# Holding q and k loads to three tiles, moving stores to GpSimd's ring, and gating transposes and scores apart

## The chip, the cores and the metric

The kernel runs on one core of a Trainium2 chip. The metric is the device time of one launch in microseconds. Thirteen runs of the kernel before gave a median of 214.38 us (213.67 to 217.96). Separate from them, one execution was profiled.

## What is computed

Attention over 4 batches, 8 heads, 768 positions and a head size of 64, with a distance bias, a local window of 96 positions and 8 global positions; its output, with the heads side by side, goes through two matrices with a "tanh shrink" between them.

```python
scores = scale * np.matmul(q, k.transpose(0, 1, 3, 2))
keep = is_global | is_local          # first 8 positions, or 0 <= row - col < 96
scores = np.where(keep, scores + bias, -1e9)
a = softmax(scores)                  # row maximum taken off, sum + 1e-9
x = (a @ v), heads side by side      # 3072 x 512
h = x @ w_in                         # 512 x 2048
out = (h - np.tanh(h)) @ w_out       # 2048 x 512
```

Inputs and output are float32; the kernel computes its products in bfloat16.

## The kernel before

**Tiles.** The 3072 rows are 24 tiles of 128. They are visited in the order `SEQ` (line 50): first the first tile of each batch, then the others. In all that follows a tile's number u is its place in this order. A tile needs its own keys (the diagonal block), and, unless it is the first of its batch, the keys of the tile before it in its batch (the other block). The global keys and values are copied into the first columns of each key tile (K, line 333) and the first rows of each value tile (V, line 360).

**Steps of one tile.** The loads of k, q and v (`load_bf`, line 232) cast to bfloat16 and are issued by GpSimd; k and q of a tile share a tile of store `kq` from the pool `bpool`, with `KQ` = 5 buffers (lines 47 and 80). k and q of tiles 0 and 1 come as float32 by SyncE and ScalarE and are cast on chip. T is the transpose of q and k: for tiles 0 to 5 TensorE does it (lines 277 and 281, `PE_T` = 6), for the others a DMA transpose that SyncE issues (`a_DT`, line 283), from `kq` into a tile `qk` of `kpool` (7 buffers). S is the scores (line 314); from tile 12 three blocks are run together (`R3`, `RUN`). E is the exponential on ScalarE (line 323), M the mask on VectorE (line 329), AV the product with v on TensorE (lines 342 and 346), R the division by the row sum on VectorE (lines 354 and 355), X the transpose of the result: TensorE to tile 8 (line 369), then a DMA transpose by SyncE (`a_DX`, line 380).

**The two matrices.** Tiles 0 to 5 are groups of one tile, the others groups of two (`groups`). m1 (line 410) multiplies a group by `w_in` in chunks; th is tanh on ScalarE (line 422), g is h - tanh(h) on VectorE (line 429). m2 (line 444) multiplies by `w_out` in four quarters for each tile, ev copies the sum out of PSUM (line 454) into a tile `ot` (4 buffers), and st stores it: `store` (line 456) is issued by ScalarE, and for the last tile by SyncE.

**What sets the order.** Each engine runs its instructions in the order in which they stand. That order is made before the build by `plan()` (line 702). Each operation is entered by `op` or `flex` with an engine, a duration, the operations that it comes after, and the buffers that it takes and gives back; `plan()` repeatedly picks the operation that can start first by these durations. DMAs get a model of two rings (`ring` and `share`, lines 724 and 725), and a table `NUDGE` (line 467) shifts single operations by hand. The durations decide only the order: on the chip an instruction waits for semaphores, that is for data and for buffers, and not for the planned time.

Progress of m1 is counted in tiles: `prog` (line 576) lists each chunk of m1 with the number of tiles that are done before it. A tile's transpose may be planned only after the last chunk with a progress of at most u - 5.5 (`AHEAD`, `go` and `late`, lines 608 and 609); its scores follow when the transpose is done.

```python
go = [key for a, key in prog if a <= u - AHEAD]
late = [("issue", ("T", u - 1)) if u else None, go[-1] if go else None]
...
op(("T", u), SP, 0.3, lambda u=u: a_DT(u), after=[rk, rq] + late, give=["kq"], dma=T_DT, slack=SLACK_DT)
```

**Queues.** GpSimd issues all loads but four in one list: the order of the early ones is `LOADS` (line 532; t is a tile's three loads, i a piece of `w_in`, o a piece of `w_out`), and later tiles follow in order. The build gives GpSimd's DMAs eight semaphores, so each issue waits for the landing of the one eight places before it. A k load also waits until its `kq` buffer is free, and everything behind it in GpSimd's list waits with it. SyncE's list holds the DMA transposes of T and X in one order, so a transpose can wait behind another's data. ScalarE issues the stores between its other work.

Of the kernel before, what the change touches and what calls it, by code (L numbers as in the profile page):

```python
# [15 lines left out]
def kernel(  # L16
# [11 lines left out]
    nc = tc.nc  # L28
# [18 lines left out]
    KQ = 5  # L47
# [33 lines left out]
    kpool = ctx.enter_context(tc.tile_pool(name="kpool", bufs=7))  # L81
# [374 lines left out]
    def store(u, part):  # L456
        lo, hi = parts(u)[part]
        eng = nc.sync if u == NU - 1 else nc.scalar
        eng.dma_start(out=out[SEQ[u] * P : (SEQ[u] + 1) * P, lo:hi], in_=ots[u][:, lo:hi])


    AHEAD = 5.5
# [4 lines left out]
    NUDGE = {  # L467
        ('AV', 21): -0.3,
        ('E', 12, 1): 0.3,
        ('E', 13, 0): 0.3,  # L470
        ('E', 13, 1): -0.6,
        ('E', 14, 1): -0.6,
        ('E', 17, 0): -0.15,
        ('E', 17, 1): -0.15,
        ('E', 18, 1): 0.15,
        ('E', 21, 1): 1.0,
        ('E', 9, 1): -0.3,
        ('M', 14, 1): 0.3,
        ('M', 20, 0): 1.0,
        ('M', 9, 1): 1.0,  # L480
        ('R', 15): 0.6,
        ('R', 9): -0.3,
        ('S', 3, 0): 0.15,
        ('S', 6, 0): 1.0,
        ('S', 7, 0): 0.6,
        ('V', 16): -0.15,
        ('V', 19): -0.6,
        ('V', 4): -0.3,
        ('X', 6): 0.15,
        ('Xe', 9): -0.3,  # L490
        ('ev', 7, 0): 1.0,
        ('g', 1, 6): 0.3,
        ('g', 11, 6): 0.6,
        ('g', 13, 14): 0.3,
        ('g', 2, 2): 0.6,
        ('g', 7, 14): 1.0,
        ('g', 7, 8): 0.6,
        ('g', 9, 2): 1.0,
        ('m1', 12, 0): 0.6,
        ('m1', 4, 4): -0.3,  # L500
        ('m1', 4, 8): -0.15,
        ('m1', 5, 0): -0.3,
        ('m1', 5, 4): -0.3,
        ('m1', 5, 8): -0.15,
        ('m1', 6, 2): 0.6,
        ('m1', 8, 6): 1.0,
        ('m1', 9, 8): 0.6,
        ('m2', 1, 2): 1.0,
        ('m2', 10, 0): 1.0,
        ('m2', 11, 0): -0.3,  # L510
        ('m2', 12, 3): 0.3,
        ('m2', 15, 1): 0.3,
        ('m2', 2, 1): 1.0,
        ('m2', 21, 1): 0.6,
        ('m2', 3, 0): 0.6,
        ('m2', 3, 2): 1.0,
        ('m2', 5, 3): 1.0,
        ('m2', 7, 1): 0.3,
        ('m2', 7, 3): 0.3,
        ('m2', 8, 0): 1.0,  # L520
        ('st', 12, 0): 0.6,
        ('st', 8, 0): 1.0,
        ('th', 6, 10): -0.6,
        ('th', 7, 10): 0.3,
        ('th', 9, 8): 0.15,
    }
    SLACK_DT, SLACK_DX = 4.0, 4.0
    WARM = (1.1, 7.0)
    COLD = 6.3
    FETCH = (15.8, 0.9)  # L530
    T_ROWS, T_LD, T_W, T_ST, T_DT, T_DX = 0.67, 0.89, 1.3, 0.7, 1.75, 0.9
    LOADS = "ttttiiitiiiotoooioitooo"
# [68 lines left out]
    for u in range(NU):  # L601
# [6 lines left out]
        go = [key for a, key in prog if a <= u - AHEAD]  # L608
        late = [("issue", ("T", u - 1)) if u else None, go[-1] if go else None]
        if u < PE_T:  # L610
            t_us = 0.47 if PLAIN <= u < ROWS else 0.24
            apart = u < APART
            for j, r in ((1, rk), (0, rq)):
                prior = [("issue", ("T1", u))] if j == 0 else []
                name = ("T1" if j else "T", u)
                op(name, PE, t_us, lambda u=u, j=j: a_T(u, j), after=[r] + late + prior,
# [5 lines left out]
        else:  # L622
            op(("T", u), SP, 0.3, lambda u=u: a_DT(u), after=[rk, rq] + late, give=["kq"], dma=T_DT, slack=SLACK_DT)
        os = (0, 1) if i else (0,)
        if u < B:
            for o in os:
# [4 lines left out]
                op(("S", u, o), PE, 0.43, lambda u=u, o=o: a_S([(u, o)]), after=after_S(u) + [("B", u, o)])  # L631
        for o in os if u >= B else ():
# [49 lines left out]
    for u in range(NU):  # L682
# [10 lines left out]
        for part in range(len(parts(u))):  # L693
# [4 lines left out]
            op(("st", u, part), SP if u == NU - 1 else ACT, 0.1 if u == NU - 1 else 0.4, lambda u=u, part=part: store(u, part), after=[("ev", u, part)],  # L698
# [3 lines left out]
    def plan():  # L702
        bufs = {"mo": 3, "kq": KQ, "p0": 3, "p1": 3,
# [40 lines left out]
        while ready or any(queues.values()):  # L744
# [13 lines left out]
            for key in ready:  # L758
                if key not in since:
                    since[key] = max([0.0] + [start[a[1]] if a[0] == "issue" else done[a] for a in ops[key]["after"]])  # L760
                if key[0] == "S" and len(ops[key]["hold"]) > 2:
                    due = min(due, since[key] + YIELD)
            for key, n in cand:
# [5 lines left out]
                via = POOL if o["eng"] is POOL else SP  # L769
                if o["dma"] and len(ring[via][1]) >= 8:  # L770
                    t = max(t, sorted(ring[via][1])[-8])
                if key not in since:
                    since[key] = max([0.0] + [start[a[1]] if a[0] == "issue" else done[a] for a in o["after"]])
# [141 lines left out]
```

The softmax here doesn't subtract the row's maximum and nothing guards it: scores larger than these inputs give would overflow.

## Time and profile before

| what | value |
|---|---|
| median of 13 runs | 214.38 us |
| the profiled execution's own time | 214.66 us |
| its span, first to last instruction | 212.9 us |
| mean granted TensorE clock | 0.998 |
| T6 to T23, the 18 DMA transposes of q and k, issue to landing | 3.0 / 9.3 / 12.2 us (least, median, most) |
| the 15 DMA transposes of x | 2.4 / 4.6 / 9.4 us |
| stores issued by ScalarE: 23 of 256 KB, median to landing | 5.9 us |
| GpSimd's k loads waiting for transposes to free `kq` | 15.1 us, 3 times |
| SyncE's sequencer waiting with a transpose for q loads | 49.9 us, 8 times |

A busy share of an engine says how long its instructions ran, not that they were at their peak; matmuls are pipelined, so the start-to-start distance of two matmuls is what one costs the stream, and "busy" of TensorE counts overlapping spans once. The chain of waits follows the last instruction back to what released it, step by step. A DMA's time is counted from its issue to the landing of all its data, so it includes the time in its queue.

### The profile page before, as it was taken

What the parts mean: (1) busy time and instruction counts of PE and PEld (TensorE: products, weight loads), DVE (VectorE), ACT (ScalarE), POOL (GpSimd) and SP (SyncE); (2) the same over time, 40 slices, a digit from 0 to 9 for tenths busy, and PEclk for the clock granted to TensorE, in tenths of its full rate; (3) what the DMA queues carried; (4) which work ended last, traced back from release to release, by engine and by line L of the source; (5) the groups of instructions that cost most, each with busy time, mean ns of one, the idle gap of its engine ahead of it and who ended that gap; (6) DMA issues with size and microseconds to landing.
All of it is one profiled execution on the core that took longest, in us unless ns stands there. A gap on an engine that the chain in (4) does not pass through costs nothing.

```text
span 212.9 us, 5322 instructions
## 1 busy us (share of the span) xinstructions
PE 205.2 (96%) x2198; PEld 145.2 (68%) x2198; DVE 131.1 (62%) x269; ACT 120.0 (56%) x184; POOL 71.9 (34%) x92
## 2 busy tenths in 40 slices
PE   7899999999599999999999999999999999999994
PEld 2679995985256867677677578757755786666754
DVE  5579895655367677385666577756655594333611
ACT  4777875553346786497358366667545673444410
POOL 8996486757146545335342700000000000000000
PEclk9999999999999999999999999999999999999999
DMA  5999999999999999999999999212373220110112
GB/s 176 185 190 177 181 203 180 186 152 151 151 165 188 185 122 189 129 183 183 151 162 178 187 122 183 50 62 64 99 94 108 77 49 0 52 51 14 38 49 100
DMA packets 106073, 27.49 MB, mean 129 GB/s; under 512 B 94656, under 2 KB 103104, under 8 KB 106048
## 3 DMA queue, kind: packets, MB, share of 16 engines
q0 software_dynamic: 74048, 13.11, 84.2%
q1 hardware_dynamic: 28144, 7.48, 27.5%
q10 hardware_dynamic: 3856, 6.56, 8.9%
q8 instruction: 17, 0.28, 0.5%
q14 instruction: 8, 0.07, 0.1%
HBM read 27.26 MB, written 6.29 MB: 158 GB/s over the span
## 4 chain that ended last, share of the span: by engine, by line
PE 90%; DMA 7%; DVE 1%; ACT 0%; issue 0%; DVEq 0%
PE ps L410 40%; PE ps L444 37%; PE ps L314 5%; DMA qk<-kq 5%; PE ps L342 3%; PE ps L346 2%; DMA kf<-in_k_dram 2%; PE ps L277 1%; PE ps L369 1%; PE ps L281 1%; PE ps L165 1%; DVE kh L296 0%; ACT qk L296 0%; DVE kq L255 0%; DVE ot L454 0%
## 5 line engine op out<-in xcount | busy, mean ns | idle before, releaser
L410 PE MATMUL ps<-xT,w_in_bf 128*128 128x256 bf16 (+1 forms) x960 | 92.9, 251 | 0.0
L444 PE MATMUL ps<-w_out_bf,g 128*128 128x512 bf16 (+3 forms) x416 | 91.2, 363 | 0.0
L410 PEld LDWEIGHTS <-w_in_bf 128*128 128x128 bf16 x960 | 77.3, 98 | 13.3 <-DMA xT<-x 0.5
L429 DVE TENSOR_TENSOR g<-ps,th 128x512 bf16<-128x512 f32 (+1 forms) x102 | 64.9, 656 | 29.0 <-ACT th L422 28.4
L422 ACT ACTIVATE th<-ps 128x512 f32<-128x512 f32 (+1 forms) x102 | 56.8, 573 | 38.0 <-PE ps L410 34.7
L444 PEld LDWEIGHTS <-g 128*128 128x128 bf16 x416 | 37.9, 98 | 33.7
L323 ACT ACTIVATE pd<-ps 128x1024 bf16<-128x1024 f32 x24 | 24.4, 1024 | 14.9 <-PE ps L314 14.9
L242 POOL DMA_DIRECT2D kq<-in_k_dram x20 | 17.8, 888 | 25.4 <-DMA qk<-kq 15.1
L236 POOL DMA_DIRECT2D vb<-in_v_dram x24 | 21.4, 891 | 13.0 <-DMA kq<-in_k_dram 3.0
L323 ACT ACTIVATE po<-ps 128x1024 bf16<-128x1024 f32 x20 | 20.3, 1024 | 6.1 <-PE ps L314 6.1
L242 POOL DMA_DIRECT2D kq<-in_q_dram x20 | 17.7, 886 | 6.2 <-DMA vb<-in_v_dram 4.4
L329 DVE TENSOR_TENSOR pd<-pd,mk 128x1024 bf16<-128x1024 bf16 x20 | 13.8, 690 | 6.4 <-ACT pd L323 6.3
L355 DVE TENSOR_TENSOR x<-ps,rden 128x512 bf16<-128x512 f32 x24 | 16.6, 691 | 0.8
L454 ACT COPY ot<-ps 128x512 f32<-128x512 f32 x16 | 9.4, 585 | 13.7 <-PE ps L444 13.7
L329 DVE TENSOR_TENSOR po<-po,mk 128x1024 bf16<-128x1024 bf16 x20 | 13.6, 686 | 2.9 <-ACT po L323 2.9
L342 PE MATMUL ps<-vb,pd 128*128 128x65 bf16 x192 | 14.1, 193 | 0.0
L342 PEld LDWEIGHTS <-pd 128*128 128x128 bf16 x192 | 12.5, 98 | 1.4 <-issue 0.2
L314 PE MATMUL ps<-qk 64*128 64x128 bf16 x288 | 10.8, 217 | 2.5 <-DMA qk<-kq 2.5
L454 DVE COPY ot<-ps 128x512 f32<-128x512 f32 (+3 forms) x10 | 5.8, 585 | 12.0 <-PE ps L444 11.9
L314 PEld LDWEIGHTS <-qk 64*128 64x128 bf16 x288 | 8.1, 94 | 7.5 <-issue 4.2
L346 PE MATMUL ps<-vb,po 128*128 128x65 bf16 x160 | 12.4, 193 | 0.0
L346 PEld LDWEIGHTS <-po 128*128 128x128 bf16 x160 | 10.4, 97 | 1.1
(48 smaller groups left out, 80.8 us busy)
## 6 DMA issues: line engine op xcount, KB each, us to landing
out_dram<-ot ACTq DMA_DIRECT2D x23, 256.0 KB, 5.9
vb<-in_v_dram POOLq DMA_DIRECT2D x24, 128.0 KB, 10.9
kq<-in_k_dram POOLq DMA_DIRECT2D x22, 128.0 KB, 11.7
kq<-in_q_dram POOLq DMA_DIRECT2D x22, 128.0 KB, 11.5
w_in_bf<-in_moe_w_in_dram POOLq DMA_DIRECT2D x8, 256.0 KB, 7.9
w_out_bf<-in_moe_w_out_dram POOLq DMA_DIRECT2D x8, 256.0 KB, 9.0
kf<-in_k_dram SPq DMA_DIRECT2D x2, 256.0 KB, 4.7
qf<-in_q_dram ACTq DMA_DIRECT2D x2, 256.0 KB, 4.0
```

Of the source, the lines that this page charges most:

```text
L236: i = nc.gpsimd.dma_start(out=v_of(u)[:, :, 0:Dh], in_=by_head)
L242: i = nc.gpsimd.dma_start(out=dst.rearrange("p (h d) -> p h d", d=Dh), in_=by_head)
L314: nc.tensor.matmul(s[:, slot(2 * p + hh), :], kT(prev_of[u] if o else u)[r, p, :], qk[u][r, 0, p, :], start=u >= B, stop=True, skip_group_ ...
L323: nc.scalar.activation(pr[u, o].rearrange("q (a h) f -> q a h f", a=2)[:, part], sc[u, o][:, part, :].rearrange("q a (h f) -> q a h f", f= ...
L329: nc.vector.tensor_tensor(out=pr[u, o], in0=pr[u, o], in1=mk[:, :, mask_of(u, o) - 1, :], op=ALU.mult)
L342: nc.tensor.matmul(dst, pr[u, 0][:, slot(h), :], v_of(u)[:, h, :], start=True, stop=last,)
L346: nc.tensor.matmul(dst, pr[u, 1][:, slot(h), :], v_of(prev_of[u])[:, h, :], start=False, stop=True,)
L355: nc.vector.tensor_tensor(out=xs[u].rearrange("q (a h) d -> q a h d", a=2), in0=t[:, :, :, 0:Dh], in1=rden.to_broadcast([P, 2, H // 2, Dh] ...
L410: nc.tensor.matmul(t[:, (f - f0) * n : (f - f0 + 1) * n], w_in_bf[j][:, c, fo : fo + P], xT[b][:, c, o : o + n], start=(c == 0), stop=(c = ...
L422: nc.scalar.activation(h_view(ths[g, f0], g, m), h_view(hs[g, f0], g, m), AF.Tanh, bias=0.0, scale=1.0)
L429: nc.vector.tensor_tensor(out=gs[b][:, f0 : f0 + m, o : o + n], in0=h_view(hs.pop((g, f0)), g, m), in1=h_view(ths.pop((g, f0)), g, m), op= ...
L444: nc.tensor.matmul(os_[u, part][:, 0 : hi - lo], gs[b][:, f, t * P : (t + 1) * P], w_out_bf[f // FJ][:, f % FJ, lo:hi], start=(f == 0), st ...
```

## The change

- `KQ` goes from 5 to 3: at most three tiles of k and q are in store between load and transpose. `kpool` goes from 7 to 8 buffers, and the planner now counts them (`qk`): T takes one, the scores that read it last give it back.
- `store` is issued by GpSimd for tiles 0 to 20, by ScalarE for tiles 21 and 22 and by SyncE for tile 23. In GpSimd's list a store stands between loads, and waits there for its eviction.
- The gate is split. T keeps 5.5 (`AHEAD_T`). Scores of tiles from 4 on get a gate of their own: they may be planned only after the chunk of m1 with a progress of at most u - 4.5 (`gate`).
- The order of the early loads (`LOADS`) changes.
- The table of nudges is emptied, and the planner's model of DMA is replaced: `fly` advances three rings (GpSimd's, SyncE's, ScalarE's) together with shares that depend on which have work, and stops them at fixed times (`FETCHES`). The durations of the engines' operations stay, but for issues of stores.

In the order that is built, TensorE has the same instructions as before in another order. GpSimd's list has three stores behind the loads of tile 9, one behind those of each of tiles 10 and 11, and from tile 13 on a store behind most tiles' loads: store 5 behind tile 13, store 6 behind 14, stores 7 and 8 behind 17, and stores 9 to 12 behind 18 to 21; stores 13 to 20 follow all loads. SyncE's list has the transposes in nearly the same order; x of tiles 10 and 17 now stand ahead of T13 and T21, and x of tile 19 ahead of x of tile 20.

```diff
--- before.py
+++ after.py
@@ -44,7 +44,8 @@
     WJ = 8
     FJ = CF // WJ
     NV = 9
-    KQ = 5
+    KQ = 3
+    NK = 8
     ROWS = 4
     APART = 4
     SEQ = [b * NQ for b in range(B)] + [t for t in range(NU) if t % NQ]
@@ -78,7 +79,7 @@
     cpool = ctx.enter_context(tc.tile_pool(name="const", bufs=1))
     stpool = ctx.enter_context(tc.tile_pool(name="stage", bufs=PLAIN))
     bpool = ctx.enter_context(tc.tile_pool(name="bpool", bufs=KQ))
-    kpool = ctx.enter_context(tc.tile_pool(name="kpool", bufs=7))
+    kpool = ctx.enter_context(tc.tile_pool(name="kpool", bufs=NK))
     ppool = ctx.enter_context(tc.tile_pool(name="ppool", bufs=3))
     xpool = ctx.enter_context(tc.tile_pool(name="xpool", bufs=3))
     tpool = ctx.enter_context(tc.tile_pool(name="tpool", bufs=NG))
@@ -455,81 +456,30 @@
 
     def store(u, part):
         lo, hi = parts(u)[part]
-        eng = nc.sync if u == NU - 1 else nc.scalar
+        eng = nc.sync if u == NU - 1 or u < BY_SP else nc.gpsimd if u < BY_POOL else nc.scalar
         eng.dma_start(out=out[SEQ[u] * P : (SEQ[u] + 1) * P, lo:hi], in_=ots[u][:, lo:hi])
 
 
-    AHEAD = 5.5
+    AHEAD, AHEAD_T = 4.5, 5.5
+    BY_POOL, BY_SP = 21, 0
     YIELD = 0.0
     HALVES = 99
     EB = 2
     INF = 1.0e9
-    NUDGE = {
...
-    }
-    SLACK_DT, SLACK_DX = 4.0, 4.0
+    NUDGE = {}
+    SLACK_DT, SLACK_DX = 1.0, 1.0
...
-    FETCH = (15.8, 0.9)
-    T_ROWS, T_LD, T_W, T_ST, T_DT, T_DX = 0.67, 0.89, 1.3, 0.7, 1.75, 0.9
-    LOADS = "ttttiiitiiiotoooioitooo"
+    FETCHES = [(15.8, 0.9), (23.0, 0.2), (31.0, 0.3)] + [(a, 0.9) for a in (40, 49, 61, 72, 83, 94, 105, 116, 127, 140)]
+    T_ROWS, T_LD, T_W, T_ST, T_DT, T_DX = 0.67, 0.89, 1.3, 0.65, 1.05, 0.55
+    RING = 5.8
+    TAIL = {POOL: 0.45, SP: 0.8, ACT: 0.8}
+    SHARE = {
+        (True, False, False): (1.0, 0, 0), (False, True, False): (0, 1.0, 0), (False, False, True): (0, 0, 1.0),
+        (True, True, False): (0.36, 0.42, 0), (True, False, True): (0.5, 0, 0.42), (False, True, True): (0, 0.5, 0.42),
+        (True, True, True): (0.3, 0.29, 0.2),
+    }
+    LOADS = "tttitiiitiiootooiiotooo"
     first, n_of = [], {"t": 0, "i": 0, "o": 0}
     for c in LOADS + "t" * NU:
         if n_of[c] < (NU if c == "t" else WJ):
@@ -587,13 +537,16 @@
             op(("mke", m, a), ACT, 0.52, lambda m=m, a=a: a_mke(m, a), after=[("mk", m, a)],
                free=[("mk", m, a)], pri=1)
 
-    run_of, blocks_of = {}, {}
+    run_of, blocks_of, gate = {}, {}, {}
     for u in range(NU):
         for o in (0,) if u < B else (0, 1):
             n = 2 * (u - R3) + o
             first_b = (u, o) if u < B else (u, 0) if u < R3 else (R3 + n // RUN * RUN // 2, n // RUN * RUN % 2)
             run_of[u, o] = ("S",) + first_b
             blocks_of.setdefault(run_of[u, o], []).append((u, o))
+
+    for u in range(B, NU):
+        gate[u] = [key for a, key in prog if a <= u - AHEAD][-1:]
 
     def after_S(u):
         return ([("Te", u, 0), ("Te", u, 1)] if u < PE_T else [("T", u)])
@@ -605,22 +558,21 @@
             flex(("cq", u), [(ACT, 0.55), (DVE, 0.6)], lambda eng, u=u: cast(u, 0, qf, eng), after=[rq], pri=-1)
             flex(("ck", u), [(DVE, 0.6), (ACT, 0.55)], lambda eng, u=u: cast(u, 1, kf, eng), after=[rk], pri=-1)
             rk, rq = ("ck", u), ("cq", u)
-        go = [key for a, key in prog if a <= u - AHEAD]
-        late = [("issue", ("T", u - 1)) if u else None, go[-1] if go else None]
+        late = [("issue", ("T", u - 1)) if u else None] + [key for a, key in prog if a <= u - AHEAD_T][-1:]
         if u < PE_T:
             t_us = 0.47 if PLAIN <= u < ROWS else 0.24
             apart = u < APART
             for j, r in ((1, rk), (0, rq)):
                 prior = [("issue", ("T1", u))] if j == 0 else []
                 name = ("T1" if j else "T", u)
-                op(name, PE, t_us, lambda u=u, j=j: a_T(u, j), after=[r] + late + prior,
+                op(name, PE, t_us, lambda u=u, j=j: a_T(u, j), after=[r] + late + prior, take=["qk"] if j else [],
                    hold=[(name, 1)] if apart or j else [], give=[] if j else ["kq"])
                 flex(("Te", u, j), [(ACT, 0.5), (DVE, 0.6 if u < ROWS else 0.34)],
                      lambda eng, u=u, j=j: a_Te(u, j, eng),
                      after=[("T1" if j and apart else "T", u)] + ([] if apart or j else [("Te", u, 1)]),
                      free=[name] if apart else [] if j else [("T1", u)])
         else:
-            op(("T", u), SP, 0.3, lambda u=u: a_DT(u), after=[rk, rq] + late, give=["kq"], dma=T_DT, slack=SLACK_DT)
+            op(("T", u), SP, 0.3, lambda u=u: a_DT(u), after=[rk, rq] + late, take=["qk"], give=["kq"], dma=T_DT, slack=SLACK_DT)
         os = (0, 1) if i else (0,)
         if u < B:
             for o in os:
@@ -628,16 +580,19 @@
                    after=biased_by + [("dT", 1) if o else None,
                                     ("issue", ("S", u - EB, 0)) if u >= EB else None],
                    hold=[(("S", u, o), 2)])
-                op(("S", u, o), PE, 0.43, lambda u=u, o=o: a_S([(u, o)]), after=after_S(u) + [("B", u, o)])
+                op(("S", u, o), PE, 0.43, lambda u=u, o=o: a_S([(u, o)]), after=after_S(u) + [("B", u, o)],
+                   give=["qk"])
         for o in os if u >= B else ():
             if run_of[u, o] != ("S", u, o):
                 continue
             bl = blocks_of["S", u, o]
             deps = [("issue", ("mk", 1, 1)), ("issue", ("mk", 2, 1))]
+            back = [w for w, ow in bl if ow and prev_of[w] >= B] + [w for w, ow in bl if ow and SEQ[w] % NQ == NQ - 1]
             for w, ow in bl:
+                deps += gate[w]
                 deps += after_S(w) + [("K", prev_of[w]) if ow and prev_of[w] >= B else None]
             op(("S", u, o), PE, 0.22 + 0.215 * len(bl), lambda bl=bl: a_S(bl), after=list(dict.fromkeys(deps)),
-               hold=[(("S", w, ow), 2) for w, ow in bl])
+               hold=[(("S", w, ow), 2) for w, ow in bl], give=["qk"] * len(back))
         for o in os:
             if u < HALVES:
                 op(("E", u, o), ACT, 0.93, lambda u=u, o=o: a_E(u, o), after=[run_of[u, o]],
@@ -695,12 +650,13 @@
             flex(("ev", u, part), alt, lambda eng, u=u, part=part: m2_e(u, part, eng),
                  after=[("m2", u, 4 * part + 3)], take=["ot"] if part == 0 else [],
                  give=["mo"] if u < EARLY2 else [], free=[("m2", u, part)], pri=1)
-            op(("st", u, part), SP if u == NU - 1 else ACT, 0.1 if u == NU - 1 else 0.4, lambda u=u, part=part: store(u, part), after=[("ev", u, part)],
+            by = SP if u == NU - 1 or u < BY_SP else POOL if u < BY_POOL else ACT
+            op(("st", u, part), by, {SP: 0.3, POOL: 0.7, ACT: 0.4}[by], lambda u=u, part=part: store(u, part), after=[("ev", u, part)],
                give=["ot"] if part == len(parts(u)) - 1 else [], dma=T_ST)
 
 
     def plan():
-        bufs = {"mo": 3, "kq": KQ, "p0": 3, "p1": 3,
+        bufs = {"mo": 3, "kq": KQ, "qk": NK, "p0": 3, "p1": 3,
                 "x": 3, "xT": NG, "g": NG, "th": 3, "ot": 4}
         avail = {n: [0.0] * c for n, c in bufs.items()}
         free = {PE: WARM[0], ACT: 3.4, DVE: 1.5, POOL: 1.0, SP: 0.7}
@@ -721,9 +677,58 @@
                 b[i : i + n] = [INF] * n
             return at, got
 
-        ring = {SP: [0.0, []], POOL: [5.8, []]}
-        share = {SP: 0.5, POOL: 0.5}
         done, start, width = {}, {}, {}
+        flying, landed, at_dma = {POOL: [], SP: [], ACT: []}, {POOL: [], SP: [], ACT: []}, [0.0]
+
+        def fly(jobs, t, t_end):
+            fin = {}
+            while t < t_end:
+                stop = [(a, n) for a, n in FETCHES if t < a + n][:1] or [(INF, 0)]
+                if stop[0][0] <= t:
+                    t = min(sum(stop[0]), t_end)
+                    continue
+                heads = [q for q in jobs if jobs[q] and jobs[q][0][1] <= t]
+                later = min([jobs[q][0][1] for q in jobs if jobs[q] and jobs[q][0][1] > t] + [t_end])
+                if not heads:
+                    t = later
+                    continue
+                rate = SHARE[tuple(q in heads for q in (POOL, SP, ACT))]
+                rate = {q: r for q, r in zip((POOL, SP, ACT), rate)}
+                dt = min([later - t] + [jobs[q][0][2] / rate[q] for q in heads])
+                dt = min(dt, stop[0][0] - t)
+                t += dt
+                for q in heads:
+                    jobs[q][0][2] -= dt * rate[q]
+                    if jobs[q][0][2] < 1e-6:
+                        key = jobs[q].pop(0)[0]
+                        fin[key] = t + TAIL[q] + ops[key]["slack"]
+            return fin
+
+        def fly_from(q, key, t, end):
+            busy = flying[POOL]
+            done.update(fly(flying, at_dma[0], t))
+            at_dma[0] = max(at_dma[0], t)
+            begin = end + (2.0 if q is POOL else 1.0)
+            if key[0] in ("T", "Xe"):
+                begin = t + (4.2 if busy else 2.2)
+            if q is POOL:
+                begin = max(begin, RING)
+            flying[q].append([key, begin, ops[key]["dma"], q])
+            landed[q].append(key)
+            done.update(fly({k: [list(j) for j in v] for k, v in flying.items()}, at_dma[0], INF))
+
+        flies = {key: any(a[0] != "issue" and ops[a]["dma"] for a in o["after"]) for key, o in ops.items()}
+
+        def due_at(key):
+            if flies[key] or key not in since:
+                since[key] = max(
+                    [0.0] + [start[a[1]] if a[0] == "issue" else done[a] for a in ops[key]["after"]]
+                )
+            return since[key]
+
+        def at_of(x):
+            return done[x] if isinstance(x, tuple) else x
+
         f1 = f2 = 0.0
         queues = {}
         for u in range(NU):
@@ -756,22 +761,17 @@
                     cand.append((qu[0], 10 ** 6 + name[1]))
...
@@ -786,7 +786,7 @@
                     if len(avail[p]) < n_p:
                         t = None
                         break
-                    t = max(t, sorted(avail[p])[n_p - 1])
+                    t = max(t, sorted(at_of(x) for x in avail[p])[n_p - 1])
                 if t is None:
                     continue
                 c = (round(t + NUDGE.get(key, 0.0), 3), o["pri"], n)
@@ -805,16 +805,7 @@
             if o["at"]:
                 done[key] = o["at"]
             elif o["dma"]:
-                via = POOL if o["eng"] is POOL else SP
-                mine, other, part = ring[via], ring[SP if via is POOL else POOL], share[via]
-                begin = max(mine[0], end + (1.0 if via is SP else 1.97))
-                both = min(max(0.0, other[0] - begin), o["dma"] / part)
-                mine[0] = begin + o["dma"] + both * (1 - part)
-                if begin < FETCH[0] <= mine[0]:
-                    mine[0] += FETCH[1]
-                other[0] += both * part
-                done[key] = mine[0] + (0.8 if via is SP else 0.45) + o["slack"]
-                mine[1].append(done[key])
+                fly_from(o["eng"], key, t, end)
             else:
                 done[key] = end + LAT[o["eng"]]
             if o["hold"]:
@@ -832,9 +823,9 @@
                     continue
                 bank[banks[label] : banks[label] + width[label]] = [done[key]] * width[label]
             for p in o["take"]:
-                avail[p].remove(min(avail[p]))
+                avail[p].remove(min(avail[p], key=at_of))
             for p in o["give"]:
-                avail[p].append(done[key])
+                avail[p].append(key if o["dma"] and not o["at"] else done[key])
             order.append((t, key))
             if key[0] == "m1":
                 queues["m1", min(key[1], EARLY)].pop(0)
```

More of the change, by code (lines that the diff above doesn't have):

```diff
@@ L466 @@
     INF = 1.0e9
-    NUDGE = {
[L468 to L525, printed above, removed]
-    }
@@ L758, in plan @@
             for key in ready:
-                if key not in since:
-                    since[key] = max([0.0] + [start[a[1]] if a[0] == "issue" else done[a] for a in ops[key]["after"]])
                 if key[0] == "S" and len(ops[key]["hold"]) > 2:
-                    due = min(due, since[key] + YIELD)
+                    due = min(due, due_at(key) + YIELD)
             for key, n in cand:
@@ L768, in plan @@
                 t = free[eng]
-                via = POOL if o["eng"] is POOL else SP
[L770 to L773, printed above, removed]
-                t = max(t, since[key])
+                if o["dma"] and len(landed[eng]) >= 8:
+                    t = max(t, done[landed[eng][-8]])
+                t = max(t, due_at(key))
                 if key[0] == "m1" and t >= due:
@@ L807, in plan @@
             elif o["dma"]:
-                via = POOL if o["eng"] is POOL else SP
-                mine, other, part = ring[via], ring[SP if via is POOL else POOL], share[via]
-                begin = max(mine[0], end + (1.0 if via is SP else 1.97))
-                both = min(max(0.0, other[0] - begin), o["dma"] / part)
-                mine[0] = begin + o["dma"] + both * (1 - part)
-                if begin < FETCH[0] <= mine[0]:
-                    mine[0] += FETCH[1]
-                other[0] += both * part
-                done[key] = mine[0] + (0.8 if via is SP else 0.45) + o["slack"]
-                mine[1].append(done[key])
+                fly_from(o["eng"], key, t, end)
             else:
```

## The prediction

> **What bounds the kernel now.** I read the page's busy row first, then the chain of waits in order of time, then TensorE's waits, then the landing times of the DMA transposes one by one.
>
> ```profile
> PE 205.2 (96%) x2198; PEld 145.2 (68%) x2198; DVE 131.1 (62%) x269; ACT 120.0 (56%) x184; POOL 71.9 (34%) x92
> ```
>
> TensorE is busy for 205.2 of 212.9 us, and the change neither adds nor removes a matmul. So whatever it brings can only come out of the other 7.7 us, and whatever it costs must show as new TensorE idle time. The chain of waits between 40 and 57 us holds the only large hole (columns: start, length, what):
>
> ```profile
> 43.46 2.69 PE ps L410 x48
> 46.18 0.14 ACT th L422
> 46.32 10.38 DMA qk<-kq
> 56.70 0.04 issue
> 56.75 0.62 PE ps L314 x16
> ```
>
> TensorE's own list of waits says the same, and after 8 us it holds this line alone:
>
> ```profile
> PE ps L314 <- DMA qk<-kq: 2.5, 1, 2.5
> ```
>
> Scores of tile 7 (S7; tiles are numbered in the order of visits) start at 56.75, when T7, its DMA transpose issued at 46.32, has landed at 56.70. Measured from matmul start to matmul start, the piece before S7 takes 3.56 instead of 0.86 us, so the hole is 2.69 us. A second, of 0.19 us, stands at 79.9 (the first L410 piece of group 7 waits for the transposed x of tile 9). The remaining idle time is start-up and the tail after the last matmul (209.86 to 212.9), which the change leaves as they are.
>
> Why T7 is slow is read from the rows of DMA:
>
> ```profile
> DMA  5999999999999999999999999212373220110112
> ...
> q0 software_dynamic: 74048, 13.11, 84.2%
> q1 hardware_dynamic: 28144, 7.48, 27.5%
> q10 hardware_dynamic: 3856, 6.56, 8.9%
> ...
> out_dram<-ot ACTq DMA_DIRECT2D x23, 256.0 KB, 5.9
> ```
>
> All 16 engines are full to 133 us, with three queues at once: GpSimd's loads (q0), SyncE's transposes (q1), ScalarE's stores (q10). Asked one at a time, T6 (issued 37.4, no store in flight) took 8.0 us; T7, T13 and T18, each beside one or two stores, took 10.4. T8 and T9 landed 4.5 and 3.6 us behind their predecessor (61.16, 64.77).
>
> **TensorE's order, and the time to win.** The pieces have fixed durations in the chain: L410 eight matmuls of 256 columns 0.87 us, sixteen of 128 columns 0.89; L444 four 0.86; scores 0.55 (16) or 0.78 (24), and 0.1 where they follow a dense piece; attention times V 0.48; x transpose 0.22. Summed in order from the first scores (7.34), before ends at 205.30. The trace ends at 209.86; of the 4.56 between, 2.88 are the two holes and 1.68 are small waits ahead of 15.4 us, where the order hardly changes. The changed order sums to 205.40 (one more scores piece behind a dense one), so without holes its last matmul ends at 205.40 + 1.68 = 207.08, and its span is 207.08 + 3.04 (tail) = 210.1 us. That is the most there is: 2.78 us, 1.3%.
>
> **Part 1: scores gated at 4.5, transposes at 5.5.** No instruction waits for a gate on the chip; it only places pieces in TensorE's list. Example: between S6 and S7 stood 5 L444 pieces and one AV (4.9 us); now 5 L444, 3 L410 of 0.89, AV and X (7.7 us). Times of need without holes, against those of before without holes: S7 56.1 (54.1), S8 59.3 (58.9), S9 64.6 (62.4), S10 72.9 (69.4), S11 76.2 (75.8), group 7's first L410 79.0 (77.2), S12 90.0 (85.6), S13 96.5 (93.9), S15 109.7 (108.8). The part gives 0.4 to 4.4 us, least at S8 and S11.
> *What is late next:* a removed hole brings every later need forward by 2.7 us. Set against the very landings of before: T7 56.70 is 0.64 late; then S8 (59.9) waits for T8 at 61.16, 1.22 more; S9 (66.5) is met; S11 (78.1) is met by T11 at 76.73; x of tile 9, which moves with AV9, is 0.4 late. At unchanged DMA the holes are 1.9 to 2.3 us, and the gain only 0.5 to 0.9.
>
> **Part 2: 21 stores from ScalarE's queue to GpSimd's.** ScalarE loses 21 issues of 0.338 us (7.1): worth nothing, it is idle 44%. GpSimd's issue of a store is not in the trace: between 0.34 (ScalarE's row) and 0.89 (a V load); nearest is a w_out load of the same 256 KB, 0.70. 21 x 0.70 = 14.7 us on an engine that is idle for 141; hidden, but what stands behind a store in its list waits for that store's eviction. Does the move speed the transposes? The Trainium skill, DMA: Bandwidth & Descriptors, section "Issuing engines are not separate DMA queues", speaks against it: transfers share the same 16 engines whoever starts them, and another issuer saves only sequencer time. By that rule T7 takes 10.4 again. The rows differ: 8.0 without a store beside it, 10.4 with. The same page ("Queues, rings and completion order") says that each engine takes turns between queue rows, which fits: three rows at work become two. No store can now move ahead of the loads already in the ring; the first three are queued behind V of tile 9 (landing about 54). I take 8.5 for T7, near T6: it lands at 54.8, ahead of S7. T8 follows by 3.6 (T9's row): 58.4, ahead of S8 at 59.3. By the rule the hole is 1.9, by the rows 0.
>
> **Part 3: three tiles of store.** The k load of tile u+3 now waits for T(u) to land. Behind it on GpSimd stand q, V, and every later load and store. Round for tile 10: T7 lands 54.8, q is issued by 55.7; with a near-empty ring a load lands 5.9 to 6.7 after issue (the two at 116 us), so q10 by 62.4. T10 at 62.4 + 8.7 (its own row) = 71.1 for S10 at 72.9. Tile 11: T8 58.4, q11 66, T11 + 8.5 to 9.9 = 75 for S11 at 76.2. x of tile 9, issued at 70.8 behind T11, + at most 8.6 = 79.4 for 79.0: 0 to 0.4. Tile 13: its transpose stands behind x of tile 10 (AV10 76.8 + 1.65 = 78.4) on SyncE, so 79.7 + 8 to 10.3 = 88 to 90 for S12 at 90.0. Tile 14 is the first whose load stands behind a late store (store 5, evicted at 73.5): k 74.4, q 82 at most, T14 92 for S13 at 96.5. Later stores (7 and 8 evicted at 89.7 and 95, 12 at 131) leave T18 and T22 over 8 us. Slack is positive everywhere, but 1 to 2 us at T10, T11, T13: cost 0, at most 1.
>
> **Part 4: order of the early loads, eighth qk buffer, no nudges.** The same bytes in another order: w_in 3 now lands where k4 did, at 18.5 to 18.9 (16.44 + 1.30 + a gap of 0.74 that k4 and q4 show), for a piece at 18.6; w_in 5 stays at 23.5 for 23.9; w_out 0 and 1 land by 26.5 for 27.1, w_out 3 at 31.7 for 32.1. Cost 0 to 0.5. The 58 nudges vanish: the planner keeps its durations of the engines, and with them before shows no TensorE wait for ScalarE, VectorE or a PSUM bank after 8 us; AV stands 3.4 to 4.2 us behind its scores in both lists. What hides them is this distance; where it fails, 0.1 to 0.3 per scores piece, 0 to 1.5 in all. I take 0.5 for all of part 4.
>
> **Sum.** The profiled execution took 214.66 us, 1.76 more than its span; the median shown is 214.38. 214.66 - 2.78 + 0.5 = 212.4, and less the 0.28 by which the profiled execution stands above the median: **212.1**.
>
> **Rivals.**
> (a) *Transposes as slow as before* (the rule's side; three buffers and stores as ring traffic change no share): holes 2.1 at S7, S8 and x9, plus 0.5: 214.38 - 2.78 + 2.6 = 214.2, no change. For it: DMA stays full, the same bytes must move by 80 us. Against: T6's 8.0.
> (b) *Slower: the ring of three buffers becomes the pace.* The buffer of tile 7 serves tiles 10 and 13, so T13 lands two rounds (a load and a transpose each) after T7: 54.8 + 2 r, for S12, which holds a block of tile 13, at 90.0. By the rows above r is 16 to 17 (71.1 - 54.8). If loads land 9.8 after issue (the q at 119.8) and transposes take 10.4, with 0.9 of issue before them, r is 21: holes of 54.8 + 42 - 90 = 6.8, and 214.38 - 2.78 + 0.5 + 6.8 = 218.9; at r = 19.5 it is 216.1. It decides from 2 r = 90 + 2.3 - 54.8, r = 18.8, where the gain is gone. For it: even five buffers left GpSimd waiting 15.1 us for transposes. Against: no ring can be long when only three tiles may be in flight.
> (c) *The change is not what its words say:* loads aren't later, since store was never what held them. Then it is (a).
>
> **Chances.** 212.1 (within 211.2 to 213.3): 0.60. (a), 213.3 to 215: 0.18, half of it faster. (b) and other new waits, over 215: 0.22. Two executions' medians tell 0.2% (0.43 us) from no change, so faster 0.67, same 0.08, slower 0.25. Range: 211.0 (all of 2.78 and a bit at start-up) to 215.6, which leaves out most of (b).
>
> **What would show it.** Right: no TensorE wait of over 0.5 us for qk after 8 us; T7 and T8 under 9.5 us; DMA digits below 9 between 60 and 133 us; POOL busy at 86 or so. Part 1 wrong: a wait of L314 for qk at S8 or S11. Part 2 wrong: T7 over 10 us. Part 3 wrong: L314 waits at S10 to S13 with k loads idle on qk just before. Part 4 wrong: L410 or L444 waiting for a weight before 45 us, or L314 for ACT or DVE. The forecast is wrong if TensorE's idle time between 8 us and its last matmul exceeds 2.9 us.

## The result and the profile after

The changed kernel takes 212.52 us in the median of 11 runs (212.47 to 212.71), against 214.54 us for the kernel before in 48 runs (213.17 to 217.96). The ratio is 0.9911, with a 95% interval of 0.9891 to 0.9932: 0.9% faster. Ratios here and below leave out runs that lie more than 1.5% above the fastest of their kernel. The profiled execution took 212.37 us, with a span of 210.6 us. The forecast was 212.1 us.

The lines below are from the page of the changed kernel; its line numbers are one higher than before's from line 49 on. Shares of queues are of 16 engines' span.

```profile
PE 205.9 (98%) x2198; PEld 145.2 (69%) x2198; DVE 130.6 (62%) x271; ACT 118.8 (56%) x182; POOL 84.1 (40%) x113
...
DMA  5999999999999999999999995993511121110012
...
q0 software_dynamic: 75728, 18.62, 92.7%
q1 hardware_dynamic: 28144, 7.48, 24.0%
q10 hardware_dynamic: 832, 1.05, 1.5%
...
out_dram<-ot POOLq DMA_DIRECT2D x21, 256.0 KB, 3.4
```

TensorE's matmuls are the same 2198, and the span has shrunk around them. The stores' bytes have moved from q10 to q0. The row of DMA is as full as before's up to 126 us (24 slices of 5.27 us), dips to 5 in one slice, and runs on to 142 us, where before's falls to 2 at 133. Both pages show 27.49 MB moved: the DMA engines have no less to do, so what changed is who waits for whom. TensorE's own waits are now these two, both before 8 us:

```profile
PE ps L393 <- DVE zero L865: 1.0, 1, 1.0
PE ps L315 <- ACT qk L297: 0.2, 1, 0.2
```

The chain of waits between 43 and 52 us (start, length, what) shows what stands where the transpose of tile 7 stood: dense work, without a hole.

```profile
43.53 2.68 PE ps L411 x48
46.21 1.73 PE ps L445 x8
47.94 0.55 PE ps L315 x16
48.49 2.69 PE ps L445 x12
51.18 0.89 PE ps L411 x16
```

T7 was issued at 46.02 and landed at 52.05, in 6.03 us instead of 10.38; S7 came only at 56.23. For the three transposes issued between 45 and 58 us (T7, T8, T9), the view of their line gives the time from issue to landing, first for before, then for after:

```profile
DMA to landing us min/median/max: 10.4/12.1/12.2
```

```profile
DMA to landing us min/median/max: 6.0/8.1/9.3
```

GpSimd's list around 46 us (start, length, instruction, and in brackets its idle time and what ended it) shows why:

```profile
45.94 0.87 POOL L243 DMA_DIRECT2D kq<-in_k_dram  x1 [5.52 <-DMA qk<-kq]
46.80 0.88 POOL L243 DMA_DIRECT2D kq<-in_q_dram  x1
47.66 0.89 POOL L237 DMA_DIRECT2D vb<-in_v_dram  x1
48.53 1.16 POOL L460 DMA_DIRECT2D out_dram<-ot  x2
50.48 0.55 POOL L460 DMA_DIRECT2D out_dram<-ot  x1 [0.80 <-DVE ot L455]
52.62 0.90 POOL L243 DMA_DIRECT2D kq<-in_k_dram  x1 [1.59 <-DMA qk<-kq]
```

With three tiles of store, GpSimd waited 5.5 us for T6 to land before it could issue the load of tile 9 (before had issued it at 41.72). The last load ahead of it, v of tile 8, landed at 49.18, and k of tile 9 at 51.67: for 2.5 us, just when T7 moved its data, no load landed. The first three stores stand behind the loads of tile 9, and landed after T7. Below, "the ring" is GpSimd's queue of DMAs that are issued and have not landed; it is called full when loads are issued far ahead, and short when few are under way.

### The profile page after: what moved, and what is told of

Read it like the earlier page. It is cut to its first block, busy times and chain, and to the rows that moved or that the text cites. A ratio compares the mean times of both kernels' runs of the same rounds, so it can differ in the third digit from the quotient of the medians.

```text
span 210.6 us, 5364 instructions
## 1 busy us (share of the span) xinstructions
PE 205.9 (98%) x2198; PEld 145.2 (69%) x2198; DVE 130.6 (62%) x271; ACT 118.8 (56%) x182; POOL 84.1 (40%) x113
## 2 busy tenths in 40 slices
DMA packets 104729, 27.49 MB, mean 131 GB/s; under 512 B 94656, under 2 KB 103104, under 8 KB 104704
## 4 chain that ended last, share of the span: by engine, by line
PE 95%; DMA 2%; DVE 1%; ACT 0%; issue 0%; DVEq 0%
PE ps L411 41%; PE ps L445 40%; PE ps L315 6%; PE ps L343 3%; PE ps L347 2%; DMA kf<-in_k_dram 2%; PE ps L278 1%; PE ps L370 1%; PE ps L282 1%; PE ps L166 1%; DVE kh L297 0%; ACT qk L297 0%; DVE kq L256 0%; DVE ot L455 0%; DVEq L297 0%
## 5 line engine op out<-in xcount | busy, mean ns | idle before, releaser
L411 PE MATMUL ps<-xT,w_in_bf 128*128 128x256 bf16 (+1 forms) x960 | 96.5, 251 | 0.0
L445 PE MATMUL ps<-w_out_bf,g 128*128 128x512 bf16 (+3 forms) x416 | 93.3, 363 | 0.0
L411 PEld LDWEIGHTS <-w_in_bf 128*128 128x128 bf16 x960 | 77.2, 98 | 16.9 <-DMA w_in_bf<-in_moe_w_in_dram 0.2
L423 ACT ACTIVATE th<-ps 128x512 f32<-128x512 f32 (+1 forms) x102 | 57.4, 574 | 53.6 <-PE ps L411 52.2
L460 POOL DMA_DIRECT2D out_dram<-ot x21 | 11.9, 568 | 88.1 <-ACT ot L455 84.4
L455 ACT COPY ot<-ps 128x512 f32<-128x512 f32 x20 | 11.7, 587 | 12.0 <-PE ps L445 11.8
L315 PE MATMUL ps<-qk 64*128 64x128 bf16 x288 | 10.8, 217 | 0.0
L347 PEld LDWEIGHTS <-po 128*128 128x128 bf16 x160 | 10.4, 97 | 0.5
```

The lines of the kernel that those rows point to most:

```text
L315: nc.tensor.matmul(s[:, slot(2 * p + hh), :], kT(prev_of[u] if o else u)[r, p, :], qk[u][r, 0, p, :], start=u >= B, stop=True, skip_group_ ...
L347: nc.tensor.matmul(dst, pr[u, 1][:, slot(h), :], v_of(prev_of[u])[:, h, :], start=False, stop=True,)
L411: nc.tensor.matmul(t[:, (f - f0) * n : (f - f0 + 1) * n], w_in_bf[j][:, c, fo : fo + P], xT[b][:, c, o : o + n], start=(c == 0), stop=(c = ...
L423: nc.scalar.activation(h_view(ths[g, f0], g, m), h_view(hs[g, f0], g, m), AF.Tanh, bias=0.0, scale=1.0)
L445: nc.tensor.matmul(os_[u, part][:, 0 : hi - lo], gs[b][:, f, t * P : (t + 1) * P], w_out_bf[f // FJ][:, f % FJ, lo:hi], start=(f == 0), st ...
```

## The experiments

The change has three parts that can be undone one at a time: the **lists** (every engine's order: gates, early loads, no nudges; the eighth buffer of `kpool` goes with them), the **stores** (ScalarE's or GpSimd's queue) and the **tiles** (five or three buffers of `kq`). In each kernel below the planner still works with its own settings, so that the order of TensorE, VectorE and SyncE is that of its parent; only the buffers of the pool or the issuing engine that the chip gets are changed. My theory was that stores out of the third queue make T7 fast enough, with the lists moving the needs. Rival 1: the lists alone do it. Rival 2: the stores alone. Rival 3: the three tiles.

**The lists alone** (`e_order`).

```diff
-    bpool = ctx.enter_context(tc.tile_pool(name="bpool", bufs=KQ))
+    bpool = ctx.enter_context(tc.tile_pool(name="bpool", bufs=5))
-        eng = nc.sync if u == NU - 1 or u < BY_SP else nc.gpsimd if u < BY_POOL else nc.scalar
+        eng = nc.sync if u == NU - 1 else nc.scalar
```

> The changed kernel with its lists unchanged, but five tiles of store for k and q and the 21 stores back in ScalarE's queue: of the change only the order of the lists is left. Theory (the DMA parts make the transposes fast, the order alone only moves the needs): T7 takes 8 to 10.5 us again, TensorE waits 1 to 2.5 us in all for transposes at S7, S8 or S11, time 213.5 to 214.5 us. Rival 1 (the order alone is enough, because scores stand later in it): T7 lands as late as before but no scores wait, 212.5 us.

Measured: 214.51 us beside 214.43 us for before, ratio 0.9986 (0.9951 to 1.002): no difference that can be told. Rival 1 falls in this form: scores do wait, and the gain is not there. T7 takes 9.0 us, T8 11.9, T9 13.4. TensorE's waits after 8 us in this execution:

```profile
PE ps L411 <- DMA w_in_bf<-in_moe_w_in_dram: 0.8, 1, 0.8
PE ps L347 <- DVE po L330: 0.5, 1, 0.5
PE ps L315 <- DMA qk<-kq: 0.5, 1, 0.5
```

The third line is S8, as expected; S7 itself, moved to 57.3 by the lists, no longer waits for a T7 that lands at 55.4. The first line is time lost early on: `w_in` 2 landed at 18.42 here and at 16.64 in the changed kernel, although nothing differs up to then. In three of the thirteen traces, of kernels with either lists, it landed at 18.0 to 18.4, in the other ten at 16.2 to 16.9; why stays open. Four of the ten executions here took 213.2 to 213.5 us, the others 214.5 and more; whether this early wait parts them is not shown. The second line I had not expected. The chain of waits leads it back to a transpose:

```profile
66.71 10.34 DMA qk<-kq
...
77.07 0.02 ACTq L460
...
77.13 0.34 ACTq L460
...
77.57 1.03 ACT po L324
...
78.62 0.70 DVE po L330
```

A store in ScalarE's list (L460) waited for T11 to land at 77.05, because the two DMAs share one of the eight semaphores of the hardware queues. The exponential of tile 10's other block stood behind it, then its mask, then AV. Where the store stands in ScalarE's list comes here from the planner's place for it in GpSimd's list, so this wait belongs to this experiment and not to every schedule. It is not small: S12 starts 2.40 us later here than in the changed kernel. Of these, 1.03 us are there already at S5 (a later start and `w_in` 2), 0.55 come at S8, and 0.82 with this store. How much the lists would bring alone, with the store elsewhere in ScalarE's list, was not run; from these figures I estimate up to 0.8 us.

**Both DMA parts with before's lists** (`e_stores_three`): the pool of the kernel before with `bufs=3`, and

```diff
-        eng = nc.sync if u == NU - 1 else nc.scalar
+        eng = nc.sync if u == NU - 1 else nc.gpsimd if u < 21 else nc.scalar
```

> The kernel before with its own lists, but three tiles of store for k and q and 21 stores issued by GpSimd: the two DMA parts without the new order. Theory: T7 lands at 52 to 54 instead of 56.7, ahead of S7 at 54.1, no wait of over 0.5 us is left, 212.3 to 213.0 us. Rival 1 (the order does it): S7 still waits over 1.5 us, 214 us or more.

Measured: 212.59 us, ratio 0.9923 (0.9894 to 0.9953). T7 landed at 53.10 and S7 came at 54.15. The new lists aren't needed for the gain.

**Only the stores** (`e_stores`: the last diff alone).

> The kernel before with its own lists, only the 21 stores moved to GpSimd. Rival 2 (stores alone, a third queue beside the transposes is what slowed T7): T7 takes 8.0 to 8.5, lands at 54.5, the wait falls from 2.7 to 0.5 us, 212.7 us. Rival 3 (the three tiles are what counts, since the ring is as full as before): T7 takes 9.5 to 10.5, wait of 2 us or more, 214 us. I hold 2 for likelier at T7, with some waits left at T8 to T11.

Measured: 212.71 us, ratio 0.9937 (0.9901 to 0.9974), ten runs from 212.32 to 215.21. T7 was issued 0.4 us earlier (45.93), took 8.63 us and landed at 54.56, close to what rival 2 said. The store that was under way beside T7 in the kernel before is this one (start, length, what):

```profile
44.12 0.35 ACTq L459 DMA_DIRECT2D out_dram<-ot  x1
```

It landed at 51.00, in the middle of T7. With the stores moved it is

```profile
47.49 0.58 POOL L459 DMA_DIRECT2D out_dram<-ot  x1
```

and landed at 57.02, behind T7; no store moved data beside T7. `e_order` fits this: its stores are ScalarE's, but the first was issued at 49.4 and landed at 58.97, and T7 took 9.0 us.

**Only the tiles** (`e_three`: `bufs=3` alone).

> The kernel before with its own lists, only the store for k and q cut from five tiles to three. Rival 3: loads of tile 9 and 10 are held until T6 and T7 land, the ring runs dry beside T7, T7 takes 6 to 7 us, no wait, 212.5 us. Rival 2: ScalarE's stores still share, T7 takes 9 or more, wait of 1.5 us or more, 213.5 us or more.

Measured: 212.90 us, ratio 0.9931 (0.9900 to 0.9962), nine runs from 212.04 to 214.26. T7 took 6.00 us although ScalarE's stores kept their queue. The three transposes T7 to T9:

```profile
DMA to landing us min/median/max: 6.0/6.8/7.1
```

So rivals 2 and 3 are both right about T7, each alone: T7 was 2.7 us late, stores take 1.75 us off it (and its issue came 0.4 us earlier), tiles 4.4 us. What is left of a hole at S7 under `e_stores` is 0.4 us. But "no wait" did not hold for the tiles alone. TensorE waited for T10, which took 9.24 us and landed at 71.15:

```profile
PE ps L314 <- DMA qk<-kq: 1.3, 1, 1.3
```

In the kernel before T10 landed no earlier (71.12), but S10 came at 72.11; with the hole at S7 gone it was needed 2.3 us sooner. Two of ScalarE's stores were under way beside it; in `e_stores_three` and its repeat, without them, T10 took 6.8 and 7.1 us. The profiled execution took 213.55 us. Four of the nine took 212.0 to 212.4, so the wait need not be in each.

**The other two corners** (`e_order_stores`: the changed kernel with `bufs=5`; `e_order_three`: the changed kernel with the stores on ScalarE).

> The changed kernel with its lists unchanged and only the store for k and q set back to five tiles. Rival 2 (stores are what counts): within 0.2 us of the changed kernel, T7 8 us or less, no wait. Rival 3 (three tiles are what counts): the ring is full beside T7 to T11, T7 9 us or more, waits of 1 to 2 us, 213.5 us or more.

> The changed kernel with its lists unchanged and only the 21 stores set back to ScalarE's queue. Rival 2: T7 takes 9 to 10 us and the waits come back, 1 us or more, 213.5 us or more. Rival 3: T7 6 to 7 us, no wait, 212.5 us or a little less, since the ends of the program wait less.

Measured: 212.47 us, ratio 0.9885 (0.9835 to 0.9934), and 212.33 us, ratio 0.9878 (0.9821 to 0.9934), four runs each; the kernel before took 215.26 us beside them, so these ratios are not to be set against the others. Neither loses anything against the changed kernel. Against the expectation of rival 3, five tiles with the new lists leave no wait although T8 and T9 take 10.2 and 11.4 us: the lists have put S8 and S9 late enough. Against rival 2, the stores back in ScalarE's queue cost nothing when the ring is short.

The eight corners side by side (us; medians, with the second measurement where there is one):

| lists | stores | tiles | T7 | T8 | T6 to T23, median | time |
|---|---|---|---|---|---|---|
| before | ScalarE | 5 | 10.4 | 12.2 | 9.3 | 214.4 to 215.3 |
| before | GpSimd | 5 | 8.6, 8.6 | 10.8, 9.4 | 9.1, 9.1 | 212.71, 212.62 |
| before | ScalarE | 3 | 6.0 | 7.1 | 6.9 | 212.90 |
| before | GpSimd | 3 | 6.9, 5.7 | 7.3, 5.8 | 6.6, 6.4 | 212.59, 212.51 |
| after | ScalarE | 5 | 9.0 | 11.9 | 9.9 | 214.51 |
| after | GpSimd | 5 | 7.2 | 10.2 | 6.8 | 212.47 |
| after | ScalarE | 3 | 5.6 | 7.9 | 6.6 | 212.33 |
| after | GpSimd | 3 | 6.0, 4.8 | 8.1, 6.8 | 5.8, 5.2 | 212.52, 212.55 |

One hole can only be removed once. Any row with at least one of the two DMA parts has the gain or most of it, and no pair of parts adds up.

The column of all 18 transposes shows something that T7 alone hides. With before's lists the stores leave the median where it was (9.3 to 9.1): they helped at T7, and T7 was where the hole stood. With the new lists and five tiles the same edit takes it from 9.9 to 6.8. There the stores also hold the loads back. While loads are still to be issued (to 135 us), GpSimd waits with a store for ScalarE's eviction, first in `e_stores`, then in `e_order_stores`:

```profile
POOL out_dram L459 <- ACT ot L454: 7.9, 2, 5.3
```

```profile
POOL out_dram L460 <- ACT ot L455: 41.7, 10, 9.1
```

With all causes it is 15 us against 46. Every load behind such a store waits with it: k of tile 10 was issued at 46.89 in `e_order` and at 50.82 in `e_order_stores`. So in the new lists the stores do in part what the three tiles do. With five tiles no run has the stores in GpSimd's queue without such a hold, so how much is due to the queue and how much to the held loads stays open. With three tiles and before's lists GpSimd waits with its stores for 1.2 us or less, and they change the median only from 6.9 to 6.6 and 6.4.

**Again on one chip** (`after_2`, `e_stores_three_2`, `e_stores_2`). The runs above were on different chips, so the changed kernel was run beside two of its parts.

> The changed kernel as it is, beside the next three on one chip. 212.5 us, no TensorE wait for a transpose, tail 3.4 us.

> The kernel before with its own lists and both DMA parts, beside the changed kernel. If the order of the lists is worth nothing once the transposes are fast: the same time within 0.2 us, 212.5 us. If it is worth slack: 0.3 to 0.6 us slower, since S7 comes at 54.1 and leaves T7 1 us, and the times spread more.

> The kernel before with only the stores moved to GpSimd, again: its first profile fell on its slowest execution (215.21 us, median 212.71). If stores alone leave the ring full and the needs close: waits of 0.3 to 2 us for transposes that change from execution to execution, median 212.5 to 213.2, a spread of over 1 us where the changed kernel has 0.3. If that profile was an outlier: no waits and a narrow spread.

Measured: 212.55 us (ratio 0.9907, 0.9883 to 0.9931), 212.51 us (0.9906, 0.9881 to 0.9931) and 212.62 us (0.9913, 0.9887 to 0.9939). With both DMA parts, before's lists are as fast as the new ones. With stores alone one wait is left:

```profile
PE ps L314 <- DMA qk<-kq: 0.4, 1, 0.4
```

Its six runs went from 212.49 to 213.10, so the 215.21 us of its first profile, with waits of 1.2 us for transposes and 1.5 us for x of tile 9, was not typical. I had expected more spread than this. Ten runs of it the first time spread over 2.9 us and eleven of the changed kernel over 0.24, but side by side on this chip the spreads are alike (0.61 and 0.71 us), so that the new lists make the times steadier is not shown.

**The tail** (`e_tail`, `e_tail_2`). From the end of the last matmul to the end of the span the changed kernel takes 3.4 us (207.20 to 210.6), 0.4 more than before. (As in the prediction, the end is taken as the last matmul's start and 0.03 us, its distance from the one ahead of it.) In the traces of the corners the tail goes with the stores alone: 3.4 us where GpSimd issues them, 3.0 where ScalarE does. SyncE, which issues the last three stores, ends the program by passing one semaphore after another; its waits for DMAs there are, in the changed kernel,

```profile
SPq L901 <- DMA out_dram<-ot: 1.1, 2, 0.7
```

and in before

```profile
SPq L910 <- DMA out_dram<-ot: 0.7, 2, 0.4
```

The edit puts six stores back into a hardware queue, at a time when all loads are done:

```diff
-        eng = nc.sync if u == NU - 1 or u < BY_SP else nc.gpsimd if u < BY_POOL else nc.scalar
+        eng = nc.sync if u == NU - 1 or u < BY_SP else nc.gpsimd if u < 15 else nc.scalar
```

> The changed kernel with stores 15 to 20 (all loads are done by then) back in ScalarE's queue. The tail after the last matmul grew from 3.04 to 3.4 us. Theory: at the end SyncE checks the semaphores of all queues one after another, 0.063 us each, in a fixed order; six more DMAs in the hardware queues turn their eight semaphores so that the last stores hold the last of the list instead of the first, and seven checks no longer follow the last landing: tail 3.0 us, 0.4 us less, 212.1 us. Rival: the tail is the landing of GpSimd's stores or noise, no change, 212.5 us.

> The changed kernel with stores 15 to 20 in ScalarE's queue, now beside the changed kernel itself. Tail theory: 0.4 us faster than it, 212.1 us. Rival (what was seen was the chip or the call): no difference.

Measured: 212.04 us (ratio 0.9866, 0.9826 to 0.9905), and beside the changed kernel 212.28 us against 212.55 (0.9899, 0.9872 to 0.9926). The ranges overlap (212.09 to 212.90 against 212.28 to 212.99), so the times alone don't prove the 0.3 us. The traces do show it. The last matmul ends at 207.31 and 207.36 and the span at 210.3 in both, tails of 3.0 us. The changed kernel on the same chip as the second ended its last matmul at 207.37 too, and its span at 210.76. The wait is that of before or shorter:

```profile
SPq L901 <- DMA out_dram<-ot: 0.6, 2, 0.4
```

This is the fastest version that was run.

## Why the prediction was right, and where it was not

- **The bound held.** "Without holes its last matmul ends at 207.08": it ended at 207.20. The needs that were summed from the list came within 0.25 us: S7 56.23 (56.1 forecast), S8 59.48 (59.3), S9 64.79 (64.6), S10 73.13 (72.9), S11 76.39 (76.2), group 7 79.16 (79.0), S12 90.18 (90.0), S15 109.88 (109.7).
- **Part 1 alone** was put at a gain of 0.5 to 0.9 us with transposes as slow as before, and rival (a), with 0.5 for part 4, at 214.2. The lists alone measured 214.51 beside 214.43: no gain, but with a wait at a store that is its own (0.82 us).
- **Part 2 was right at T7, from a thin row.** The step took 8.5 us for T7 from T6's row, against a rule by which moving the stores changes nothing. With only the stores moved T7 took 8.63 and 8.62, so at T7 row beat rule. But T10 of the kernel before, beside three stores, took only 8.7 us, and over all 18 transposes the stores alone changed the median from 9.3 to 9.1 us, near the rule's "nothing". With three tiles the stores' queue changed T7 from 5.60 to 6.03 or 4.80 us with the new lists and from 6.00 to 6.92 or 5.68 with the old, up or down. That T7 was the transpose that held TensorE, and the one that the stores sped up, was luck as well as reading. The issue of a store on GpSimd was put at 0.70 us and measures 0.58.

```profile
L460 POOL DMA_DIRECT2D out_dram<-ot x21: 540/579/609, 48.5 to 193.5; - x21
```

- **Part 3 is the step that failed.** It was entered as "cost 0, at most 1": loads come later, so needs may be missed. I looked only at what the wait makes late. The sum has no term for what it makes early, and that is the largest effect on T7 (6.00 us alone). T10, put at 8.7 us in the round, took 5.3. At T7's issue seven loads were under way in before and five in the changed kernel; the first packet of T7 moved 3.6 us after its issue in before, 1.3 in the changed kernel, 1.4 with the tiles alone and 3.0 with the stores alone. The cost was real too: with the tiles alone S10 waited 1.3 us for T10. The forecast came out all the same, since part 2 already removed the whole hole in the sum and the hole can't go twice.
- **Rival (b) stayed away.** T10 landed 15.8 us after T7 (16 to 17 by the rows). The second round was longer: T13 landed 18.1 us after T10, so a round took 17.0 on average, under the 18.8 at which the gain would be gone. (In the text of (b), 19.5 gives 215.9, not 216.1.)
- **Part 4 and the tail.** The 0.5 us set aside for early waits was 0.12: `w_in` 3 landed at 18.73 for a piece at 18.78. The tail, which I said the change leaves alone, took 0.4. These two errors of some 0.4 us cancelled in the sum: for the profiled execution it gave 212.38 us, and 212.37 was measured. That is closer than the terms deserve.
- **One of the signs was wrong.** DMA digits below 9 between 60 and 133 us were to show a short ring. They stay at 9 to 126 us in the changed kernel, and one slice of 5 follows, though T7 and T8 are already faster at 46 to 56 us. The row tells whether packets are in flight, not how long a newcomer waits; the time from issue to landing does.

The median is 0.4 us above the forecast, and all of that is the last step of the sum. It took off 0.28 us because before's profiled execution stood above its median; that of the changed kernel stands 0.15 below.

## What to carry to other kernels

A prefetch that runs far ahead is not free when transfers on the critical path share its engines: cutting it from five tiles to three took 4.4 us off the transpose that counted and 2.4 off the median of 18. Moving stores into the loads' own queue took 1.75 us off that one transpose and left the median alone, unless the stores also held back the loads behind them. When two parts of a change remove the same wait, test each alone before crediting either, and never add them. When a hole goes, look at the next need: it comes earlier by the same amount. And sum the work in the list first: here it gave the end to 0.12 us, and told that no part could bring more than 2.8.

## What was not expected of the hardware

- The end of a program depends on which semaphores its last DMAs hold. In these kernels SyncE passes them in a fixed order, 0.06 us apart in the trace. In the changed kernel the last store to land had the second of the hardware queues' eight semaphores in this order, and six more followed after its landing; in before one followed, in `e_tail` and `e_tail_2` none. Tails: 3.4, 3.02 and 2.96 us.
- A store can hold ScalarE for a transpose that it has nothing to do with, through a shared semaphore (in `e_order` until T11 landed, some 0.8 us on TensorE's path). GpSimd's stores have semaphores of their own.
- The same transpose, T7, depends on what stands beside it: 10.4 us with a full ring and a store that lands in its middle, 8.6 to 9.0 with a full ring and no such store, 7.2 where stores hold the next loads back, 4.8 to 6.9 with three tiles. T22, issued at 148.2 in before when loads were done, took 3.0.
